# Batch 0's last inverse stage moves into the hand-written order of the transform's last three steps

## Chip, cores and metric

The kernel runs on one NeuronCore of a Trainium2 chip. The metric is device microseconds of one execution, lower is better. TensorE (PE) multiplies, VectorE (DVE) and ScalarE (ACT) take results out of PSUM and do elementwise work, GpSimd (POOL) does one subtraction, and SyncE (SP) issues all DMA transfers. Each engine works through its own instructions in order, and SP's queue is also in order: an instruction that waits holds up everything behind it on its engine.

## What is computed

```python
def _attn_ref(x, w_r, w_i, b_r, b_i):            # x: 8 x 3136 x 256
    X = np.fft.rfft(x, axis=1)
    Yr = X.real @ w_r - X.imag @ w_i + b_r
    Yi = X.real @ w_i + X.imag @ w_r + b_i
    Yr = np.sign(Yr) * np.maximum(np.abs(Yr) - 0.01, 0.0)     # Yi the same
    return np.fft.irfft(Yr + 1j * Yi, n=3136, axis=1)

def _moe_ref(x, w_in, conv_w, w_out):            # w_in: 256 x 1024
    h = np.maximum(x @ w_in, 0.0)
    conv = sum(conv_w[k] * shifted(h, k) for k in range(3))   # 3 taps along the sequence
    return (h * sigmoid(conv)) @ w_out

out = _moe_ref(_attn_ref(x, ...), ...)
```

## The kernel before

There are two parts. **The transform** splits the Fourier transform of length 3136 = 49 x 64 into two matmul stages each way. Stage 1 transforms blocks of the input and goes through DRAM (`sc1`). The rest is a pipeline over 50 items (`n_it`), an item being a batch and a group of four frequencies. In step `it` of the loop, PE does stage 2 of item `it` (`stage2`, 16 matmuls into `ps_s2`), the complex mix of item `it-1` (`mix`, 36 matmuls into `ps_mx0..2`), and stage 3 of item `it-3` (`stage3`, 12 matmuls into `ps_s3`). Each operand is split into a high and a low part, so DVE and ACT make pairs (`fh`/`fl`, `sh`/`sl`) between the matmuls. `threshold` of item `it-2` is a chain ACT `r`, DVE `v`, ACT `sh`, POOL `sl`, which stage 3 then reads. Stage 3's result is copied by ACT to `z1` and stored by SP to DRAM (`sc2`). The loop runs three steps past the last item to drain: `range(n_it + 3)`. The order of PE, DVE and ACT in this loop is the order in which the code is written (`manual_schedule`); SP, and everything after the loop, is ordered by a scheduler when the kernel is built.

**Stage 4**, the last inverse stage, makes a batch in eight pieces (`stage4`, n = 0 to 7). A piece loads two blocks `z2` from `sc2` (two DMAs of 200 KB), does 32 matmuls of 64x49 (they are 64 in the trace), and puts the result into a batch's `yh` (ACT, L520) and `yl` (DVE, L521). `new_y` clears the two edge columns of `yh` and `yl` by four memsets (L497, L498). There are two such pairs, `y_a` for even and `y_b` for odd batches.

**The FFN** runs over 28 chunks of 896 positions (two halves of 448), each with eight blocks f of the hidden size. `up` (L533) makes `ps_h`, ACT's relu gives `h`, then the taps `c` (ACT L540 or DVE L538, then DVE L542 twice), sigmoid (ACT L543), product (DVE L544) and the pair `gh`/`gl`. `down` (L561) accumulates four blocks later into `acc`. Stage 4 of the next batch is put between the blocks, a piece at f = 1, 4 and 7.

In this version the transform's pools stand in one stack `ab`, which is closed before stage 4's pools (`zio` with three `z2` buffers, `psh` with two PSUM buffers of two banks, shared by stage 4 and `ps_h`) are opened in the same memory. All eight pieces of batch 0 and the first two of batch 1 are written ahead of the FFN; the other six of batch 1 go between its blocks.

Of the kernel before, what the change touches and what calls it, by code (L numbers as in the profile page):

```python
# [100 lines left out]
def spectral_ffn_kernel(ctx: ExitStack, tc: tile.TileContext, x, w_r, w_i, b_r, b_i,  # L101
# [19 lines left out]
    with ExitStack() as ab:  # L121
        stg = ab.enter_context(tc.tile_pool(name="stg", bufs=1))
        wbp = ab.enter_context(tc.tile_pool(name="wbp", bufs=2))
        s1p = ab.enter_context(tc.tile_pool(name="s1p", bufs=2))
        c1 = ab.enter_context(tc.tile_pool(name="c1", bufs=1))
        a2p = ab.enter_context(tc.tile_pool(name="a2p", bufs=3))
        cmx = ab.enter_context(tc.tile_pool(name="cmx", bufs=1))
# [257 lines left out]
        with tc.tile_pool(name="hx", bufs=1, reuse_waits="tile") as hx:  # L385
# [22 lines left out]
        with tc.issue_after(ld.ins):  # L408
# [5 lines left out]
        ab.enter_context(tc.manual_schedule(engines={mybir.EngineType.PE}))
        ab.enter_context(tc.issue_after(ld.ins))
        wkf, wk, cab, io = [ab.enter_context(tc.tile_pool(name=nm, bufs=n, reuse_waits="tile"))
                            for nm, n in (("wkf", 2), ("wk", 2), ("cab", 1), ("io", 2))]
# [8 lines left out]
        ab.enter_context(tc.manual_schedule(engines={mybir.EngineType.DVE, mybir.EngineType.Activation}))  # L426
        for it in range(n_it + 3):
# [45 lines left out]
            if 0 <= it - 3 < n_it:  # L473
                stage3(*items[it - 3], ss.pop(it - 3))
# [18 lines left out]
    def new_y(b):
        y = [(y_a, y_b)[b % 2].tile([P, NT, SW], F32R, name=nm) for nm in ("yh", "yl")]
        for q in y:
            qf = q.bitcast(F32)
            nc.vector.memset(qf[:, :, 0:1], 0.0)  # L497
            nc.vector.memset(qf[:, :, S + 1:S + 2], 0.0)  # L498
        return y

    def stage4(b, n, y):

        js, t = slice(n // NT * JG, (n // NT + 1) * JG), n % NT
        z2 = zio.tile([P, JG, P], F32, name="z2")
        z2v = sc2[b].rearrange("(j o c) u e -> o (c u) j e", o=2, c=2)
        for o in range(2):
            nc.sync.dma_start(z2[o * R2:o * R2 + KI], z2v[o, :, js, t * P:(t + 1) * P])
        ps = psh.tile([P, 2, 512], F32, name="ps_s4", tag="ps_h")
        for j in range(JG):
            for o in range(2):  # L510
                rows = slice(o * R2, o * R2 + KI)
                for c in range(2):
                    half = slice(c * R2, (c + 1) * R2)
                    nc.tensor.matmul(ps[half, o, j * R:(j + 1) * R], z2[rows, j, half], i2[rows, :], start=(j == 0), stop=(j == JG - 1),  # L514
                                     skip_group_check=True)
        src = ps[:, :, 0:JG * R].rearrange("p o (j m) -> p o m j", j=JG)

        def view(q):
            return q[:, t, 1:S + 1].rearrange("p (m o j) -> p o m j", o=2, j=H)[:, :, :, js]
        nc.scalar.copy(view(y[0]), src)  # L520
        nc.vector.tensor_tensor(view(y[1]), src, view(y[0].bitcast(F32)), op=ALU.subtract)  # L521
# [69 lines left out]
    n_st = NCH * NF
    for st in range(n_st + LAG):
        if st < n_st:
            ci, f = divmod(st, NF)
            hv = [divmod(2 * ci + a, NH) for a in range(2)]
            if f == 0:
                nb = hv[1][0] + 1
                if nb < B and nb not in ys and hv[0][0] == hv[1][0]:
                    ys[nb] = new_y(nb)
                    todo = [(nb, jg) for jg in range(NPC)]  # L600
            gs[st] = up(f, [(ys[b], a * CH) for b, a in hv])
            if todo and f in (1, 4, 7):
# [29 lines left out]
```

## Time and profile before

| | |
|---|---|
| median of 3 runs | 1738.86 us (1737.77 to 1741.54) |
| the profiled execution | 1738.14 us, of which its span 1736.3 us |
| mean granted TensorE clock | 0.985 |
| PE busy | 1690.5 us (97%) |
| DVE busy | 1471.0 us (85%) |
| ACT busy | 1198.4 us (69%) |
| POOL busy | 118.6 us (7%) |

Times in the profile are microseconds from the span's start. A row of a timeline gives start, duration, engine, line, operation, output and inputs, and in brackets how long the engine had been idle and what ended that. The chain of work that ended last is followed back from the last instruction, at each step to what released it. A row of the table by windows gives, for a stretch of time, the busy time of each engine with its instructions in parentheses, then the clock that PE was granted (1.00 is full), the mean busy share of the 16 DMA engines and the GB/s they moved. Waits are put down to the last of the things waited for.

### The profile page before, as it was taken

The page shows a single profiled execution, that of the slowest core. Times are in us where ns is not written, and L with a number is a line of the kernel's source. Part 1 is how long each engine was busy: PE and PEld are TensorE (multiplying, and loading weights), DVE is VectorE, ACT ScalarE, POOL GpSimd, SP SyncE. Part 2 cuts the span into 40 slices and gives each one's busy share as a digit, 9 for nine tenths or more (in the row PEclk, how much of TensorE's full clock was granted, in tenths as well). Part 3 has the DMA queues.
Part 4 walks back from the last instruction along what each step waited for, and adds up shares of the span by engine and source line. Part 5 has one row for each costly group of instructions (what it writes and reads, how often), then busy time and mean ns, then how long its engine had stood idle before and what let it go on. Part 6 is the DMA issues. An engine that isn't in the chain of part 4 may idle for free.

```text
span 1736.3 us, 35086 instructions
## 1 busy us (share of the span) xinstructions
PE 1690.5 (97%) x14944; PEld 1552.5 (89%) x14944; DVE 1471.0 (85%) x1757; ACT 1198.4 (69%) x1565; POOL 118.6 (7%) x54
## 2 busy tenths in 40 slices
PE   5999999999997999999999999999999999999999
PEld 2778888888986999999999999999999999999998
DVE  2788988898993988888888898888888888888887
ACT  2567677767663877777777677777777777777776
POOL 0122222222230000000000000000000000000000
PEclk7999999999996999999999999999999999999999
DMA  7877777667435110111111111111101111100001
GB/s 229 256 236 243 229 227 239 223 203 250 142 106 130 39 41 22 31 51 51 52 53 53 38 41 51 51 41 51 51 22 42 51 51 42 51 22 22 22 22 43
DMA packets 134604, 165.87 MB, mean 96 GB/s; under 512 B 9166, under 2 KB 112590, under 8 KB 134448
## 3 DMA queue, kind: packets, MB, share of 16 engines
q1 hardware_dynamic: 134448, 163.62, 30.7%
q8 instruction: 118, 1.93, 0.5%
q14 instruction: 38, 0.31, 0.1%
HBM read 86.01 MB, written 77.59 MB: 94 GB/s over the span
## 4 chain that ended last, share of the span: by engine, by line
PE 93%; DMA 4%; DVE 2%; issue 1%; ACT 1%; SPq 0%; DVEq 0%; ACTq 0%
PE acc L561 32%; PE ps_h L533 32%; PE ps_mx L328 11%; PE ps_s L256 5%; PE ps_s L300 5%; PE ps_s L514 4%; PE ps_s L360 3%; DMA z<-sc 1%; DMA wm_raw<-in_w_i_dram 1%; DMA t<-in_fwd_dram 1%; DVE v L336 0%; DMA sc<-a 0%; PE ps_s1h L273 0%; DMA xr<-in_x_dram 0%; DVE p L332 0%
## 5 line engine op out<-in xcount | busy, mean ns | idle before, releaser
L561 PE MATMUL acc<-wout,gh 128*128 128x256 f32 x3136 | 567.7, 281 | 1.5 <-ACT gh L547 1.5
L533 PE MATMUL ps_h<-yh,win 128*128 128x450 f32 x1792 | 550.4, 368 | 0.0
L542 DVE SCALAR_TENSOR_TENSOR c<-h,cw,c 128x896 f32<-128x896 f32 x448 | 513.4, 1148 | 26.7 <-ACT c L540 24.5
L561 PEld LDWEIGHTS acc<-wout,gh 128*128 128x128 f32 x3136 | 491.3, 188 | 10.4 <-ACT gh L547 1.9
L561 PE MATMUL acc<-wout,gl 128*128 128x256 f32 x1568 | 437.0, 280 | 0.0
L533 PEld LDWEIGHTS ps_h<-yh,win 128*128 128x128 f32 x1792 | 339.2, 189 | 25.8
L535 ACT ACTIVATE h<-ps_h 128x900 f32<-128x900 f32 x224 | 207.1, 925 | 209.9 <-PE ps_h L533 209.9
L533 PE MATMUL ps_h<-yl,win 128*128 128x450 f32 x896 | 329.7, 368 | 0.0
L544 DVE TENSOR_TENSOR c<-h,c 128x896 f32<-128x896 f32 x224 | 243.9, 1089 | 70.1 <-ACT c L543 69.6
L561 PEld LDWEIGHTS acc<-wout,gl 128*128 128x128 f32 x1568 | 293.6, 188 | 0.1
L548 DVE TENSOR_TENSOR gl<-c,gh 128x896 fp32r<-128x896 f32 x224 | 243.2, 1089 | 41.4 <-ACT gh L547 40.5
L547 ACT CAST gh<-c 128x896 fp32r<-128x896 f32 x224 | 211.6, 945 | 60.9 <-DVE c L544 60.5
L543 ACT ACTIVATE c<-c 128x896 f32<-128x896 f32 x224 | 214.0, 955 | 52.8 <-DVE c L542 51.8
L328 PE MATMUL ps_mx<-wmix_hi,fl 128*128 128x256 f32 x600 | 185.1, 308 | 2.7 <-DVE fl L310 2.7
L328 PE MATMUL ps_mx<-wmix_hi,fh 128*128 128x256 f32 x600 | 183.5, 306 | 0.7 <-DVE v L336 0.5
L533 PEld LDWEIGHTS ps_h<-yl,win 128*128 128x128 f32 x896 | 169.6, 189 | 11.1
L540 ACT ACTIVATE c<-h,cw 128x896 f32<-128x896 f32 x168 | 175.1, 1042 | 1.8
L328 PE MATMUL ps_mx<-wmix_lo,fh 128*128 128x256 f32 x600 | 168.4, 281 | 0.0
L350 POOL TENSOR_TENSOR sl<-v,sh 128x1024 fp32r<-128x1024 f32 x50 | 118.4, 2368 | 407.7 <-PE ps_s L360 249.0
L336 DVE TENSOR_TENSOR v<-ps_mx,p 64x512 f32<-64x512 f32 x200 | 137.4, 687 | 2.9
L300 PEld LDWEIGHTS ps_s<-t,a 128*128 128x128 f32 (+1 forms) x800 | 99.4, 197 | 37.0 <-issue 26.3
L328 PEld LDWEIGHTS ps_mx<-wmix_hi,fh 128*128 128x128 f32 x600 | 113.2, 189 | 19.1 <-issue 17.4
(84 smaller groups left out, 1861.0 us busy)
## 6 DMA issues: line engine op xcount, KB each, us to landing
z<-sc SPq DMA_DIRECT2D x128, 200.0 KB
xr<-in_x_dram SPq DMA_DIRECT2D x63, 392.0 KB
a<-sc SPq DMA_DIRECT2D x48, 512.0 KB
sc<-z SPq DMA_DIRECT2D x48, 512.0 KB
out_dram<-o SPq DMA_DIRECT2D x27, 896.0 KB
sc<-a SPq DMA_DIRECT2D x56, 392.0 KB
sc<-ha SPq DMA_DIRECT2D x8, 392.0 KB
win_bits<-in_moe_w_in_dram SPq DMA_DIRECT2D x4, 512.0 KB
```

Source lines behind the costliest of these rows:

```text
L300: nc.tensor.matmul(ps[:, k], a2[0:rows, k, t * P:(t + 1) * P], t2[0:rows, u, :], start=(k == 0), stop=(k == UG - 1), skip_group_check=True)
L328: nc.tensor.matmul(ps[c][:, k, :], lt, rh, start=(n == 0), stop=(n == len(mm) - 1))
L336: nc.vector.tensor_tensor(v[dst, :, k, :], ps[c][src], p1[src, c], op=ALU.add)
L533: nc.tensor.matmul(ps[:, a, 0:CH + 2], lt, rh, start=(n == 0), stop=(n == len(mm) - 1))
L535: nc.scalar.activation(h, ps[:, :, 0:CH + 2], AF.Relu)
L540: nc.scalar.mul(c, h[:, :, 0:CH], cw[:, 0, f:f + 1])
L542: nc.vector.scalar_tensor_tensor(c, h[:, :, k:k + CH], cw[:, k, f:f + 1], c, op0=ALU.mult, op1=ALU.add)
L543: nc.scalar.activation(c, c, AF.Sigmoid)
L544: nc.vector.tensor_tensor(c, h[:, :, 1:CH + 1], c, op=ALU.mult)
L547: nc.scalar.copy(gh, c)
L548: nc.vector.tensor_tensor(gl, c, gh.bitcast(F32), op=ALU.subtract)
L561: nc.tensor.matmul(acc[m // 2][:, m % 2, :], lt[:, sl], rh[:, f, :], start=(f == 0 and n == 0 and m % 2 == 0), stop=(f == NF - 1 and n == ...
```

## The change

The transform's pools are put on two sides of SBUF and PSUM. Those that are done when the last stage 2 is done (weights' staging, stage 1, `a2`; `ps1`, `ps2`) are on the left and closed early; the others (mix, threshold, stage 3) are on the right. Stage 4's `zio` (now five buffers) and `y_a` take the early pools' place during step `n_it - 1`, and SP gets the loads of pieces 0 to 4 there. Piece 0 is put between the mix's matmuls of that step, with a PSUM tile `ps_z` of its own. The loop runs to `n_it + 1`; what the last two steps did is written out behind it, with pieces 1 to 7 between. Batch 1's first two pieces go into the FFN's order with the other six. `ps_mx1` is now the lowest of the mix's three PSUM banks, in the place that `psh`'s second buffer will take. `y_b`'s `yl` now lies over `z1`, `i1_lo` and the mix's weights; before, it lay over `i1_lo`, `z1` and the end of `i1_hi`. All addresses in SBUF move, and the scratch for dynamic DMA is 4 KB instead of the default.

```diff
+ZB = 5
...
+    def load_z2(zio, b, n):
+        js, t = slice(n // NT * JG, (n // NT + 1) * JG), n % NT
+        z2 = zio.tile([P, JG, P], F32, name="z2")
+        z2v = sc2[b].rearrange("(j o c) u e -> o (c u) j e", o=2, c=2)
+        for o in range(2):
+            nc.sync.dma_start(z2[o * R2:o * R2 + KI], z2v[o, :, js, t * P:(t + 1) * P])
+        return z2
+
+    def stage4(z2, n, y, ps):
...
+        nc.scalar.copy(view(y[0]), src)
+        yield None
+        nc.vector.tensor_tensor(view(y[1]), src, view(y[0].bitcast(F32)), op=ALU.subtract)
+        yield None
...
+    with ExitStack() as late:
+        early, ps_early, ps_mid, ps_late, order = [late.enter_context(ExitStack()) for _ in range(5)]
...
-        ps1 = ab.enter_context(tc.tile_pool(name="ps1", bufs=1, space=PSUM))
-        ps2 = ab.enter_context(tc.tile_pool(name="ps2", bufs=2, space=PSUM))
-        psm = ab.enter_context(tc.tile_pool(name="psm", bufs=1, space=PSUM))
-        psa = ab.enter_context(tc.tile_pool(name="psa", bufs=1, space=PSUM))
+        ps1 = ps_early.enter_context(tc.tile_pool(name="ps1", bufs=1, space=PSUM))
+        ps2 = ps_early.enter_context(tc.tile_pool(name="ps2", bufs=2, space=PSUM))
+        psa = ps_late.enter_context(tc.tile_pool(name="psa", bufs=1, space=PSUM, side="right"))
+        psm = ps_mid.enter_context(tc.tile_pool(name="psm", bufs=1, space=PSUM, side="right"))
...
-        for it in range(n_it + 3):
+        zs = []
+        for it in range(n_it + 1):
...
             some(two, 2)
+            if it == n_it - 1:
+                early.close()
+                zio, y_a = pool("zio", ZB), pool("y_a")
+                zs += [load_z2(zio, 0, n) for n in range(ZB)]
+            if it == n_it:
+                some(head, 1)
...
+            if it == n_it - 1:
+                ps_early.close()
+                first_psh = ExitStack()
+                ps_z = first_psh.enter_context(tc.tile_pool(name="psz", bufs=1, space=PSUM, reuse_waits="tile"))
+                ys = {0: new_y(y_a)}
+                head = stage4(zs[0], 0, ys[0], ps_z.tile([P, 2, 512], F32, name="ps_z"))
+                some(head, 1)
             some(mx, 64)
...
+        first_psh.close()
+        ps_mid.close()
+        psh = pool("psh", 2, space=PSUM)
+        def to_y(n):
+            q = stage4(zs[n], n, ys[0], psh.tile([P, 2, 512], F32, name="ps_s4", tag="ps_h"))
+            yield next(q)
+            if n + ZB < NPC:
+                zs.append(load_z2(zio, 0, n + ZB))
+            yield from q
+        zs.append(load_z2(zio, 0, ZB))
+        some(to_y(1), 2)
+        stage3(*items[n_it - 3], ss.pop(n_it - 3))
+        some(to_y(2), 2)
+        th = threshold(vs.pop(n_it - 1)[0])
+        ss[n_it - 1] = next(th)
+        q = to_y(3)
+        some(q, 1)
+        some(th, 1)
+        some(q, 1)
+        some(th, 1)
+        stage3(*items[n_it - 2], ss.pop(n_it - 2))
+        some(to_y(4), 2)
+        some(to_y(5), 2)
+        some(to_y(6), 2)
+        some(to_y(7), 2)
+        stage3(*items[n_it - 1], ss.pop(n_it - 1))
...
-    for jg in range(NPC):
-        with tc.high_priority(offset=HP):
-            stage4(0, jg, ys[0])
-    ys[1] = new_y(1)
-    for jg in range(2):
-        stage4(1, jg, ys[1])
-    todo = [(1, jg) for jg in range(2, NPC)]
+    todo = []
...
-    nc = _bacc.Bacc("TRN2", target_bir_lowering=False, num_devices=1)
+    nc = _bacc.Bacc("TRN2", target_bir_lowering=False, num_devices=1, dynamic_dma_scratch_size=4096)
```

How the instructions then stand is shown at three places. On PE, in words: before, the last mix is followed by stage 3 of the third-last, second-last and last item, with the 32 matmuls of batch 0's pieces mixed in two at a time, and then two pieces of batch 1. Now it is the last mix, piece 1, stage 3 of the third-last item, pieces 2 and 3, stage 3 of the second-last, pieces 4 to 7, stage 3 of the last item, and then the FFN. From the FFN's first matmul on, PE's order is the same but for the two pieces, which come in the third chunk.

ACT from the threshold of the second-last item on (`sh`; `r` is a threshold's first step, `z` the copy of stage 3's result, `yh` a piece of stage 4). Before:

```order
L349 CAST sh<-v 128x1024
L362 COPY z_5724<-ps_s_5711 128x1024
L345 ACTIVATE r<-v,small 128x1024
L349 CAST sh<-v 128x1024
L520 CAST yh<-ps_s_5855 128x2x49x8
L520 CAST yh<-ps_s_5817 128x2x49x8
L362 COPY z_5747<-ps_s_5734 128x1024
L520 CAST yh<-ps_s_5893 128x2x49x8
L520 CAST yh<-ps_s_5931 128x2x49x8
L362 COPY z_5763<-ps_s_5750 128x1024
```

Now, from the threshold of the third-last item on:

```order
L394 CAST sh<-v 128x1024
L151 CAST yh<-ps_z 128x2x49x8
L407 COPY z_5729<-ps_s_5716 128x1024
L390 ACTIVATE r<-v,small 128x1024
L394 CAST sh<-v 128x1024
L151 CAST yh<-ps_s_5795 128x2x49x8
L407 COPY z_5846<-ps_s_5833 128x1024
L151 CAST yh<-ps_s_5849 128x2x49x8
L390 ACTIVATE r<-v,small 128x1024
L151 CAST yh<-ps_s_5891 128x2x49x8
L394 CAST sh<-v 128x1024
L407 COPY z_5942<-ps_s_5929 128x1024
```

Before, no piece stood ahead of the last item's `sh`, and two ahead of the copy of the second-last item's stage 3 (`z_5747`). Now four pieces stand ahead of that copy (`z_5942`), and piece 3 stands between `r` and `sh` of the last threshold.

DVE at the clearing of batch 1's `yh` and `yl` (MEMSET). Before:

```order
L521 TENSOR_TENSOR yl<-ps_s_5893,yh 128x2x49x8
L521 TENSOR_TENSOR yl<-ps_s_5931,yh 128x2x49x8
L497 MEMSET yh 128x2
L498 MEMSET yh 128x2
L497 MEMSET yl 128x2
L498 MEMSET yl 128x2
L521 TENSOR_TENSOR yl<-ps_s_5969,yh 128x2x49x8
```

Now:

```order
L153 TENSOR_TENSOR yl<-ps_s_6050,yh 128x2x49x8
L589 TENSOR_SCALAR c<-h,cw 128x896
L160 MEMSET yh 128x2
L161 MEMSET yh 128x2
L160 MEMSET yl 128x2
L161 MEMSET yl 128x2
L593 SCALAR_TENSOR_TENSOR c<-h,cw,c 128x896 x3
L595 TENSOR_TENSOR c<-h,c 128x896
```

The four memsets stood between batch 0's fourth and fifth piece; now they stand behind all eight, between the first two instructions of the FFN's first block. The memset of `yl` waits, then as now, for the last store of `z1`, over which `yl` lies.

SP's queue from the third-last store of stage 3's result on (`sc<-z`, 512 KB) with the loads of pieces (`z<-sc`, two of 200 KB to a piece; `sc_0` is batch 0's, `sc_1` batch 1's). Before:

```order
L364 DMA sc_7_72<-z_5724 128x1024
L507 DMA z_5928<-sc_0_65 50x8x128
L507 DMA z_5966<-sc_0_65 50x8x128
L507 DMA z_5928<-sc_0_65 50x8x128
L507 DMA z_5966<-sc_0_65 50x8x128
L364 DMA sc_7_72<-z_5747 128x1024
L507 DMA z_6004<-sc_0_65 50x8x128
L507 DMA z_6042<-sc_0_65 50x8x128
L507 DMA z_6004<-sc_0_65 50x8x128
L507 DMA z_6042<-sc_0_65 50x8x128
L364 DMA sc_7_72<-z_5763 128x1024
```

Now:

```order
L409 DMA sc_7_72<-z_5846 128x1024
L134 DMA z_5883<-sc_0_65 50x8x128 x2
L134 DMA z_6184<-sc_1_66 50x8x128 x2
L409 DMA sc_7_72<-z_5942 128x1024
L134 DMA z_6297<-sc_1_66 50x8x128 x2
L134 DMA z_6477<-sc_1_66 50x8x128 x2
L134 DMA z_6607<-sc_1_66 50x8x128 x2
L134 DMA z_6789<-sc_1_66 50x8x128 x2
L409 DMA sc_7_72<-z_6098 128x1024
```

Between the last two stores stood the loads of two pieces of batch 0; now it is four pieces of batch 1, which the FFN needs later.

More of the change, by code (lines that the diff above doesn't have):

```diff
@@ L118, in spectral_ffn_kernel @@
     mlam, warm = small[:, 0:1], small[:, 1:2]
[L121 to L127, printed above, removed]
+    JG = 8
+    NPC = H // JG * NT
@@ new lines, in stage4, with view @@
+    def stage4(z2, n, y, ps):
+        js, t = slice(n // NT * JG, (n // NT + 1) * JG), n % NT
+        for j in range(JG):
+            for o in range(2):
+                rows = slice(o * R2, o * R2 + KI)
+                for c in range(2):
+                    half = slice(c * R2, (c + 1) * R2)
+                    nc.tensor.matmul(ps[half, o, j * R:(j + 1) * R], z2[rows, j, half], i2[rows, :], start=(j == 0), stop=(j == JG - 1),
+                                     skip_group_check=True)
+        src = ps[:, :, 0:JG * R].rearrange("p o (j m) -> p o m j", j=JG)
+        def view(q):
+            return q[:, t, 1:S + 1].rearrange("p (m o j) -> p o m j", o=2, j=H)[:, :, :, js]
+        nc.scalar.copy(view(y[0]), src)
+        yield None
+        nc.vector.tensor_tensor(view(y[1]), src, view(y[0].bitcast(F32)), op=ALU.subtract)
+        yield None
@@ new lines, in new_y @@
+    def new_y(yp):
+        y = [yp.tile([P, NT, SW], F32R, name=nm) for nm in ("yh", "yl")]
+        for q in y:
+            qf = q.bitcast(F32)
+            nc.vector.memset(qf[:, :, 0:1], 0.0)
+            nc.vector.memset(qf[:, :, S + 1:S + 2], 0.0)
+        return y
+    with ExitStack() as late:
+        early, ps_early, ps_mid, ps_late, order = [late.enter_context(ExitStack()) for _ in range(5)]
+        stg = early.enter_context(tc.tile_pool(name="stg", bufs=1))
+        wbp = early.enter_context(tc.tile_pool(name="wbp", bufs=2))
+        s1p = early.enter_context(tc.tile_pool(name="s1p", bufs=2))
+        c1 = early.enter_context(tc.tile_pool(name="c1", bufs=1))
+        a2p = early.enter_context(tc.tile_pool(name="a2p", bufs=3))
+        pool("top", 1, late, side="right").tile([P, 80], F32, name="pad")
+        cmx = late.enter_context(tc.tile_pool(name="cmx", bufs=1, side="right"))
@@ L262, in stage1_head @@
         def stage1_head(xs, b=0):
-            with tc.tile_pool(name="ha", bufs=1, reuse_waits="tile") as ha:
+            with tc.tile_pool(name="ha", bufs=1, side="right", reuse_waits="tile") as ha:
                 for jc, xr in enumerate(xs):
@@ L269, in stage1_head @@
                         if k < 3:
-                            ps = psm.tile([K1, 2, D], F32, name="ps_s1h", tag=f"ps_mx{k}")
+                            ps = psm.tile([K1, 2, D], F32, name="ps_s1h", tag=f"ps_mx{(1, 0, 2)[k]}")
                         else:
@@ L315, in mix @@
             fh, fl = xs
-            ps = [psm.tile([K2, UG // 2, D], F32, name=f"ps_mx{c}") for c in range(3)]
+            ps = {c: psm.tile([K2, UG // 2, D], F32, name=f"ps_mx{c}") for c in (1, 0, 2)}
             p1 = wk.tile([K2, 2, UG // 2, D], F32, name="p1", bufs=1)
@@ L384, in spectral_ffn_kernel @@
         load_f1()
-        with tc.tile_pool(name="hx", bufs=1, reuse_waits="tile") as hx:
+        with tc.tile_pool(name="hx", bufs=1, side="right", reuse_waits="tile") as hx:
             xh = []
@@ L413, in spectral_ffn_kernel @@
                 ask()
[L414 to L417, printed above, removed]
+        order.enter_context(tc.manual_schedule(engines={mybir.EngineType.PE}))
+        order.enter_context(tc.issue_after(ld.ins))
+        io, cab, wk, wkf = [pool(nm, n, late, side="right") for nm, n in (("io", 2), ("cab", 1), ("wk", 2), ("wkf", 2))]
         cab.tile([P, 56], F32, name="pad")
-        wkf.tile([P, 56], F32, name="pad", bufs=1)
         wk.tile([P, 72], F32, name="pad", bufs=1)
+        wkf.tile([P, 8], F32, name="pad", bufs=1)
         i1_hi = cab.tile([K2, U + 2, KQ], F32R, name="i1_hi")
@@ L425, in spectral_ffn_kernel @@
         xs, vs, ss, i1s = {}, {}, {}, {}
-        ab.enter_context(tc.manual_schedule(engines={mybir.EngineType.DVE, mybir.EngineType.Activation}))
-        for it in range(n_it + 3):
+        order.enter_context(tc.manual_schedule(engines={mybir.EngineType.DVE, mybir.EngineType.Activation}))
+        zs = []
+        for it in range(n_it + 1):
             xs[it], vs[it - 1] = [], []
@@ L472, in spectral_ffn_kernel @@
                 held[:] = [0] * (next(background, None) == "act")
-            if 0 <= it - 3 < n_it:
+            if it == n_it:
+                break
+            if it >= 3:
                 stage3(*items[it - 3], ss.pop(it - 3))
@@ L493, in new_y @@
[L493 to L521, printed above, removed]
@@ L523, in up @@
+    y_b.tile([P, 32], F32, name="pad")
+    pso = pool("pso", space=PSUM)
     def up(f, halves):
@@ L603, in spectral_ffn_kernel @@
                 b, jg = todo.pop(0)
-                stage4(b, jg, ys[b])
+                for _ in stage4(load_z2(zio, b, jg), jg, ys[b], psh.tile([P, 2, 512], F32, name="ps_s4", tag="ps_h")):
+                    pass
         if st >= LAG:
```

20 lines of the change are left out of this document (7 added, 13 removed).

## Prediction, made before the changed kernel ran

> **What bounds the kernel now.** I read the page first: how much of the time PE works, and where not.
>
> ```profile
> PE 1690.5 (97%) x14944; PEld 1552.5 (89%) x14944; DVE 1471.0 (85%) x1757; ACT 1198.4 (69%) x1565; POOL 118.6 (7%) x54
> PE   5999999999997999999999999999999999999999
> PEclk7999999999996999999999999999999999999999
> ```
>
> PE is the bound almost everywhere; besides the start there is one dent, the thirteenth slice (521 to 564 us). That is the place of the change. The table by windows shows it, with a stretch of the FFN for comparison (PE busy first, then PEld, DVE, ACT, POOL; behind them granted clock, DMA share and GB/s):
>
> ```profile
> 510.00:515.00 5.00, 3.67 (x28) 3.16 (x27) 4.94 (x8) 1.96 (x2) 1.92 (x1) 1.00 0.07 27
> 525.00:530.00 5.00, 2.48 (x86) 2.23 (x89) 1.72 (x2) 1.52 (x2) 1.52 (x1) 0.76 0.82 212
> 540.00:545.00 5.00, 2.63 (x75) 2.34 (x69) 1.95 (x4) 1.70 (x2) 0.00 (x0) 0.50 0.36 89
> 555.00:560.00 5.00, 5.00 (x43) 4.52 (x38) 0.97 (x1) 1.23 (x2) 0.00 (x0) 0.66 0.73 158
> 570.00:650.00 80.00, 80.00 (x813) 75.67 (x812) 73.69 (x74) 60.23 (x69) 0.00 (x0) 1.00 0.14 38
> ```
>
> Up to 515 DVE has no gap (4.94 of 5.00). Then nobody is full, and PE runs at half clock. From 570 on PE has no gap. The chain of waits says what the dent is made of:
>
> ```profile
> 509.26 1.30 PE ps_s L360 x11
> ...
> 523.08 5.38 DMA z<-sc
> 528.51 3.08 PE ps_s L514 x95
> ...
> 532.36 5.66 DMA z<-sc
> ...
> 541.44 4.68 DMA z<-sc
> ...
> 555.80 6.32 PE ps_h L533 x24
> ...
> 567.35 1.22 PE acc L561 x8
> 568.57 4.93 PE ps_h L533 x24
> ...
> 575.14 1.08 PE ps_s L514 x64
> ```
>
> Stage 4 alternates load (4.7 to 5.7 us) and matmuls (3.08 us at half clock), since three `z2` buffers come free only when PE has read them. The FFN starts at 555.80; its first two blocks take 6.32 us cold (4.93 us warm, at 568.57), and its first `down` starts at 567.35. From there PE is the chain, so what the change is worth is the shift of that `down`, plus what is added to PE behind it.
>
> **The new order, step by step.** Up to 510 us the orders are the same. Durations of what follows, by groups (mean ns), and DVE's own timeline:
>
> ```profile
> L521 DVE TENSOR_TENSOR yl<-ps_s,yh 128x784 fp32r<-128x784 f32 x64 | 61.8, 971 | 18.9 <-ACT yh L520 18.9
> L347 DVE SCALAR_TENSOR_TENSOR v<-v,r 128x1024 f32<-128x1024 f32 x50 | 61.0, 1220 | 1.3 <-ACT r L345 1.3
> L520 ACT CAST yh<-ps_s 128x784 fp32r<-128x784 f32 x64 | 58.4, 920 | 21.1 <-PE ps_s L514 21.1
> L345 ACT ACTIVATE r<-v,small 128x1024 f32<-128x1024 f32 x50 | 58.4, 1167 | 2.6 <-DVE v L336 2.5
> L349 ACT CAST sh<-v 128x1024 fp32r<-128x1024 f32 x50 | 52.6, 1051 | 69.7 <-DVE v L347 69.4
> L350 POOL TENSOR_TENSOR sl<-v,sh 128x1024 fp32r<-128x1024 f32 x50 | 118.4, 2368 | 407.7 <-PE ps_s L360 249.0 <-ACT sh L349 152.7 <-PE ps_s L300 5.9
> L362 ACT COPY z<-ps_s 128x1024 f32<-128x1024 f32 x50 | 50.5, 1010 | 25.2 <-PE ps_s L360 22.9 <-issue 1.2 <-DMA sc<-a 0.5
> ```
>
> ```profile
> 511.73 0.69 DVE L310 TENSOR_TENSOR fl<-d,fh 128x512 fp32r<-128x512 f32 x1
> 512.33 2.81 DVE L336 TENSOR_TENSOR v<-ps_mx,p 64x512 f32<-64x512 f32 x4
> 515.24 1.29 DVE L332 TENSOR_TENSOR p<-ps_mx,bias 128x512 f32<-128x512 f32 x2
> ...
> 540.90 0.06 DVE L497 MEMSET yl<- 128x2 f32 x1 [6.25 <-DMA sc<-z]
> ...
> 561.36 2.34 DVE L542 SCALAR_TENSOR_TENSOR c<-h,cw,c 128x896 f32<-128x896 f32 x2
> ```
>
> Neighbours on an engine overlap by about 0.1 us, so in a row each counts so much less. A piece is 1.08 us on PE, a stage 3 is 1.4 us (1.30 for 11 of its 12).
>
> Piece 0 costs nothing: PE has its 1.08 us free, since the next mix waits for `fl` (done 512.42) in any case. Its `yl` puts 0.97 us on DVE, which is full. DVE then reads: `v` to 515.3, `yl` 0 to 516.25, `p` to 517.4, threshold `v` to 518.6, the last four `v` to 521.3. PE: last mix done 516.85, piece 1 to 518.0, third-last stage 3 to 519.4. Piece 2 needs `psh`'s second buffer, over `ps_mx1`, so it waits for DVE's 521.3 and ends at 522.5. Now ACT and DVE set the pace: ACT `yh` 2 to 523.4, `r` to 524.5, `yh` 3 to 525.3; DVE `yl` 2 to 524.4, threshold `v` to 525.8, `yl` 3 to 526.7. PE: piece 3 to 523.6, stage 3 to 525.0, piece 4 to 526.1, piece 5 (after `yl` 3) to 527.85. ACT: `sh` to 526.9, `z` to 527.75, `yh` 4 to 528.55, `yh` 5 to 529.4; `yl` 4 to 529.55. PE: piece 6 from there to 530.75, piece 7 to 531.85, last stage 3 to 533.25. POOL's `sl` (2.37 us behind `sh`: 522.2 and 529.4) is never last. The FFN starts at 533.3 (both `psh` buffers are read by 533.8). That is 22.5 us earlier. The loads don't delay it: the first loads were issued from 480.15 on (row below), some 0.4 to 0.7 us each, and pieces 0 to 4 need no more than 490 (an estimate: ten at that pace, and some waits); piece 7's, the latest, is issued at 522.6 (when piece 2 is read) and is needed at 530.7; the longest load in the chain took 5.66.
>
> PE has 11.8 us of work in these 16.4, 72%, as in 510 to 515 (3.67 of 5.00), where the clock stayed 1.00. So I take the first two blocks warm: 4.93 instead of 6.32, done at 538.2, **23.9 us earlier**.
>
> **The new wait.** Relu of the first block is done at 536.8 and DVE's first tap at 537.55. Then come the memsets of batch 1, which wait for the last `z` store. It was the same wait that held DVE for 6.25 us to 540.90, with nothing urgent behind it. Now all of the FFN's DVE work is behind it. The store is issued when ACT has copied the last stage 3, at 534.35, behind four pieces of batch 1.
>
> ```profile
> 480.15 3.49 SPq L507 DMA_DIRECT2D z<-sc  x5
> ...
> 535.53 0.34 SPq L364 DMA_DIRECT2D sc<-z  x1
> 551.00:557.00 6.00, 5.29 (x131) 4.92 (x132) 2.00 (x3) 1.82 (x2) 0.00 (x0) 0.50 0.73 159
> 533.00:540.00 7.00, 4.31 (x109) 3.87 (x110) 1.46 (x4) 1.29 (x2) 0.00 (x0) 0.74 0.75 191
> ```
>
> The first row is SP's issue of the first pieces, the second of the last store. The first window holds loads of pieces alone: 159 GB/s, so 2 x 204.8 KB take 2.6 us. The second holds two pieces and then the store: 1.34 MB at 191 GB/s. The store issued at 535.53 was in at 540.90, 5.4 us later and 0.9 behind the last byte. Now: the second-last store is issued at 527.8 and moves from about 529.5; behind it come four pieces (4 x 2.6 = 10.4) and the last store. A store adds about 1.4 us (the second window's 7.0, less 2 x 2.6 for its pieces, less 0.4 at its edges). So the last byte moves at 529.5 + 10.4 + 2.8 = 542.7, and the store is in at 543.6, the memsets done at 543.7. Bounds: 539.7, if the queue is no longer than before (534.35 + 5.4), and 546, if the mix moves at 191 GB/s and everything ahead is 1.5 us late. I take 543.7, since the loads ahead are four and not two. DVE so waits **6.2 us** (2.2 to 8.5).
>
> From the taps' start to the first `down` it was 567.35 - 561.36 = 6.0 us; that chain through DVE and ACT is the same. First `down`: 543.7 + 6.0 = 549.7 instead of 567.35. PE meanwhile does a piece and one more block, to 541.8, and then has nothing for 7.9 us.
>
> **The clock.** Windows of 3.4 us, laid where the granted clock changes:
>
> ```profile
> 517.60:521.00 3.40, 1.97 (x67) 1.64 (x67) 2.73 (x5) 2.48 (x3) 2.07 (x1) 1.00 0.14 55
> 521.00:524.40 3.40, 2.75 (x95) 2.49 (x87) 1.23 (x1) 2.05 (x3) 0.54 (x2) 1.00 0.41 143
> 524.40:527.80 3.40, 0.99 (x32) 0.74 (x32) 1.86 (x2) 2.12 (x3) 2.12 (x1) 0.98 0.78 179
> 527.80:531.20 3.40, 2.69 (x94) 2.69 (x96) 0.00 (x0) 0.00 (x0) 0.00 (x0) 0.50 0.59 181
> 555.00:558.40 3.40, 3.40 (x35) 3.04 (x30) 0.97 (x1) 0.91 (x1) 0.00 (x0) 0.51 0.73 154
> ```
>
> After 1.97 busy of 3.40 the clock stayed, after 0.99 it was halved, and after a full window it came back. So 7.9 us of idling halve it, and `down` begins cold. Before, PE worked without a gap from 553.85 and was warm at 558.4: 4.6 us at half speed, which is 2.3 us lost (at most twice 3.4, so 3.4 lost; nothing, if the wait is short). The Trainium skill, "TensorE: Matmul & The Clock Gate", section "Part 1: The HAM clock gate", has the same window of about 3.4 us, free-running, but lets only an idle window halve the clock. The trace is stricter: 0.99 busy did not save it. By the page the stretch of pieces, with no gap over 2.1 us, could not lose its clock at all, and the second rival below would have no chance.
>
> **Added to PE behind the first `down`:** two pieces of batch 1 in the third chunk, 2 x 1.08 = 2.2 us, in full, since PE has no gap there. Their 0.97 and 0.92 us on DVE and ACT lie in their gaps (73.69 and 60.23 of 80).
>
> **Sum:** -22.5 (FFN starts earlier) - 1.4 (warm blocks) + 6.2 (memset) + 2.3 (clock) + 2.2 (pieces) = **-13.2 us**. The profiled execution was 1738.14, so 1724.9; the median is 0.7 above it, so 1725.6. At nothing I cost: piece 0 on PE (covered by the wait for `fl`; without it 1.08 us); the new addresses and the scratch, which change no instruction; the earlier loads of pieces 2 to 4 (1.2 MB more around 490, with 10 us to spare).
>
> **Rivals.** (1) The store is in sooner. If no longer behind than before, 539.7, then DVE waits 2.2 and PE is idle for 3.9 us, which may keep the clock: -22.5 - 1.4 + 2.2 + 2.2 = -19.5, 1719.4. For it: store and loads together reached 191 GB/s, not 159. Against: twice the loads ahead. (2) The clock falls between the pieces. There PE waits for DVE and ACT about 2 us at a time, and one window with a third of work would do. Then three pieces cost 1 us more each (3.08 for 95 matmuls, against 1.08 for 64) and the first blocks 1.4: -13.2 + 4.4 = -8.8, 1730.0. Against: 1.97 of 3.40 was enough. (3) Slower than before. All tiles lie elsewhere, and if that slowed DVE in the FFN, DVE could become the bound:
>
> ```profile
> L542 DVE SCALAR_TENSOR_TENSOR c<-h,cw,c 128x896 f32<-128x896 f32 x448 | 513.4, 1148 | 26.7 <-ACT c L540 24.5
> ```
>
> DVE has 6.3 of 80 us free, so up to 8.6% more on each of its instructions is covered; every per cent above adds 0.01 x 0.92 x 1180 us = 11 us. From 9.8% on that eats the 13.2 us; at 11% it is 26 us, 1752. Nothing in the trace shows a duration that depends on the address.
>
> **Chances.** Forecast 0.50, (1) 0.24, (2) 0.18, (3) 0.03, and 0.05 that (2) and a late store come together, some 1734 to 1737. The range reaches from (1) to (2) with a us or so on each side for the spread of runs and for 0.05 us here and there in the steps: 1718.5 to 1731.5. A measurement here can tell 0.2%, 3.5 us. Faster by more: 0.93; within: 0.04; slower: 0.03.
>
> **What would show it.** Right: first FFN matmul near 533; in its first block a DVE memset that waited about 6 us for the store; PE idle for about 8 us before the first `down` near 550, then half clock for some 4 us; third chunk 2.2 us longer. Wrong: no wait at the memset (1); clock 0.50 between 518 and 533 (2); longer DVE means in the FFN (3); or a piece that waits for its load, which I excluded.

## The result, and the profile after

The changed kernel takes 1725.22 us (median of 4 runs, 1723.02 to 1726.18) against 1738.32 before: ratio 0.9923 [0.9902, 0.9944], 13.1 us faster. The forecast was 1725.6 us. The profiled execution took 1724.63 us. One execution, the profiled one of the run `again` below, was in a disturbed state and took 3954 us; no trace of it is used.

The page after, first the same lines that were shown of before:

```profile
PE 1686.4 (98%) x14944; PEld 1548.2 (90%) x14944; DVE 1470.7 (85%) x1757; ACT 1199.6 (70%) x1565; POOL 118.7 (7%) x54
PE   5999999999998999999999999999999999999998
PEclk8999999999998999999999999999999999999999
```

The dent in the thirteenth slice is an 8 instead of a 7. The windows of the stretch (PE, PEld, DVE, ACT, POOL busy, then granted clock, DMA share, GB/s):

```profile
520.00:525.00 5.00, 3.32 (x133) 3.06 (x131) 3.66 (x5) 3.79 (x5) 2.36 (x1) 0.81 0.65 194
525.00:530.00 5.00, 5.00 (x99) 4.78 (x96) 2.42 (x3) 3.31 (x5) 2.11 (x1) 0.51 0.71 169
530.00:535.00 5.00, 2.48 (x139) 2.20 (x135) 2.93 (x3) 2.62 (x3) 0.25 (x1) 0.84 0.76 201
535.00:540.00 5.00, 5.00 (x67) 4.82 (x68) 0.98 (x1) 1.37 (x2) 0.00 (x0) 0.50 0.71 155
570.00:650.00 80.00, 80.00 (x874) 75.32 (x873) 72.29 (x72) 59.17 (x71) 0.00 (x0) 1.00 0.20 55
```

PE was given half clock for much of 523 to 540, which the forecast had only as its second rival. The chain of work that ended last, from the third-last stage 3 (L405) to the first `down` (L612):

```profile
518.88 1.61 PE ps_s L405 x12
520.49 1.67 issue
522.15 2.92 PE ps_s L145 x128
525.07 2.86 PE ps_s L405 x12
527.93 1.94 PE ps_s L145 x64
...
531.86 1.48 PE ps_s L145 x75
533.34 1.52 issue
534.87 1.76 PE ps_s L145 x40
...
537.85 6.36 DMA z<-sc
544.21 1.31 issue
545.52 0.06 DVE yl L160
...
551.03 1.22 PE acc L612 x8
```

and DVE's and SP's timelines around the last `z` store (L409) and batch 1's memsets (L160):

```profile
529.88 9.13 SPq L134 DMA_DIRECT2D z<-sc  x8
540.58 0.34 SPq L409 DMA_DIRECT2D sc<-z  x1
543.30 0.69 DVE L589 TENSOR_SCALAR c<-h,cw 128x896 f32<-128x896 f32 x1 [4.74 <-ACT h L586]
545.52 0.06 DVE L160 MEMSET yl<- 128x2 f32 x1 [1.51 <-issue]
```

So the alternation of loads and matmuls is gone, as the change says. But the last store went out at 540.58 and not at 534.35, DVE waited 1.5 us for it and not 6.2, the first block of the FFN was not 22.5 us earlier but 16.5, and the first `down` came at 551.03 (forecast 549.7) with a warm PE. The chain puts the memset's wait down to a load (`z<-sc`) that was in at 544.21; the last of the store's own landings is at 545.41, 0.1 us ahead of the memset, and `free_store` below shows that the store is what it waited for. The total agreed; its terms did not. Two theories were open. **C**: what counts is PE's own lateness, so each us lost at half clock in the stretch is lost to the end, and the agreement is luck. **F** (a floor): the first `down` follows the landing of the last store, whose time is set by the loads around it, and PE may be early or late ahead of it at no price.

Single executions also differ before the change is reached: the last `fl` starts at 511.73 before and at 512.47 here (510.22 to 512.47 in all the profiles below), and keeps that offset from 250 us on. So places in the stretch are given as distances from that `fl`. `down` stands for the first one:

| kernel | clock below 1.00 in the stretch | first FFN matmul | memset's wait | `down` | from `down` to the end |
|---|---|---|---|---|---|
| before | most of it | +44.0 | | +55.6 | 1169.0 |
| forecast | no | +21.6 | 6.2 | +38.0 | 1173.5 |
| after | 13.7 us | +26.8 | 1.5 | +38.6 | 1171.8 |
| `after_again` | 6.8 | +24.1 | 3.2 | +37.1 | 1173.3 |
| `mx2_low` | 10.2 | +24.7 | 2.5 | +38.1 | 1174.5 |
| `twice` | 10.2 | +26.5 | 0.5 | +37.6 | 1171.8 |
| `zb3` | 10.2 | +28.0 | none | +39.1 | 1171.8 |
| `hold` | no | +21.5 | 10.4 | +38.7 | 1174.0 |
| `late_b1` | 6.8 | +24.4 | 0.8 | +34.9 | 1171.8 |
| `free_store` | 3.4 | +22.9 | none | +33.4 | 1171.8 |
| `free_again` | 6.8 | +24.2 | none | +34.5 | 1171.8 |
| `free_hold` | 3.4 | +24.6 | none | +35.0 | 1171.8 |
| `all_three` | 13.7 | +26.1 | none | +36.5 | 1171.8 |

The rest of the document argues from this table; its columns are read from the timelines of each profiled execution, the clock from the records of the granted clock, which change in steps of 3.41 us. "None" means that the memset did not wait for a store.

### The profile page after: what moved, and what is told of

It reads as the page before. It is cut to its first block, busy times and chain, and to the rows that moved or that the text cites. A ratio compares the mean times of both kernels' runs of the same rounds, so it can differ in the third digit from the quotient of the medians.

```text
span 1722.9 us, 35081 instructions
## 1 busy us (share of the span) xinstructions
PE 1686.4 (98%) x14944; PEld 1548.2 (90%) x14944; DVE 1470.7 (85%) x1757; ACT 1199.6 (70%) x1565; POOL 118.7 (7%) x54
## 4 chain that ended last, share of the span: by engine, by line
PE 93%; DMA 2%; DVE 2%; issue 1%; ACT 0%; SPq 0%; DVEq 0%; ACTq 0%
PE acc L612 33%; PE ps_h L584 32%; PE ps_mx L373 11%; PE ps_s L301 5%; PE ps_s L345 5%; PE ps_s L145 4%; PE ps_s L405 4%; DMA t<-in_fwd_dram 1%; DMA sc<-a 0%; DMA z<-sc 0%; DVE v L381 0%; DMA sc<-ha 0%; DVE fl L351 0%; DMA a<-sc 0%; DVE p L377 0%
## 5 line engine op out<-in xcount | busy, mean ns | idle before, releaser
L612 PE MATMUL acc<-wout,gh 128*128 128x256 f32 x3136 | 567.8, 281 | 2.5 <-ACT gh L598 2.5
L584 PE MATMUL ps_h<-yh,win 128*128 128x450 f32 x1792 | 549.7, 368 | 0.0
L593 DVE SCALAR_TENSOR_TENSOR c<-h,cw,c 128x896 f32<-128x896 f32 x448 | 513.2, 1147 | 26.5 <-ACT c L591 24.3
L612 PEld LDWEIGHTS acc<-wout,gh 128*128 128x128 f32 x3136 | 490.8, 188 | 11.4 <-ACT gh L598 2.9
L612 PE MATMUL acc<-wout,gl 128*128 128x256 f32 x1568 | 436.8, 280 | 0.0
L612 PEld LDWEIGHTS acc<-wout,gl 128*128 128x128 f32 x1568 | 293.6, 188 | 0.1
```

Source lines behind the costliest of these rows:

```text
L584: nc.tensor.matmul(ps[:, a, 0:CH + 2], lt, rh, start=(n == 0), stop=(n == len(mm) - 1))
L593: nc.vector.scalar_tensor_tensor(c, h[:, :, k:k + CH], cw[:, k, f:f + 1], c, op0=ALU.mult, op1=ALU.add)
L612: nc.tensor.matmul(acc[m // 2][:, m % 2, :], lt[:, sl], rh[:, f, :], start=(f == 0 and n == 0 and m % 2 == 0), stop=(f == NF - 1 and n == ...
```

## Experiments

**The changed kernel again, and three single edits.**

> The changed kernel once more, beside the next three on one chip: 1725 us, ratio 0.992 to the kernel before. Both theories below expect in its trace what the first trace had: half clock from about 523 to 530 and 533 to 540, first FFN matmul near 539, the memset of batch 1's yl waiting 1 to 2 us for the last store, first down near 551. If the clock falls in other windows here, the stretch of pieces should move by some us, but theory F (floor: DMA is busy from 520 to 544 with batch 1's loads, so the last store lands near 544 to 546 however early it is issued, and the first down follows 5.5 to 6 us later) expects the first down to stay at 549 to 551.5; theory C (clock: what the stretch loses at half clock is lost to the end) expects the first down to move with the first FFN matmul.

Measured: 1725.31 us, ratio 0.9925 [0.9911, 0.9938], the same as in the first measurement. What the two theories expected of its trace is left to `after_again` below.

```diff
-    ... f"ps_mx{(1, 0, 2)[k]}" ...        for c in (1, 0, 2)}
+    ... f"ps_mx{(2, 0, 1)[k]}" ...        for c in (2, 0, 1)}
```

> Only the mix's three PSUM banks change places: ps_mx2 (read first by DVE) lies in the lowest, so piece 2 waits for the p of the last mix instead of its last v. Piece 2 should start right behind the third-last stage 3, 1.6 us earlier, and the window in which the clock fell (about 1.75 us busy of 3.4) is then busy for 2.8 or more. Theory C: the clock stays 1.00 to 533, the first FFN matmul comes at 534 to 535 instead of 539, and the time falls by 4 to 5 us (1720 to 1721). Theory F: the same in the stretch, but the memset then waits 5 to 6 us instead of 1.5, PE idles longer before the first down, and the time falls by 0 to 1.5 us (1724 to 1725).

Measured: 1723.74 us (1720.04 to 1726.26), 0.9914 [0.9901, 0.9928]. The wait of 1.67 us ahead of piece 2 is gone, and a wait of 1.55 us ahead of piece 3, for DVE's `yl`, stands in its place: DVE sets the pace, whichever bank is free. The clock fell here too (10.2 us of the stretch), so the run doesn't decide between the theories. Its profiled execution shows the forecast's clock term: PE idle for 3.5 us ahead of the first `down`, and then cold. Windows of the clock's own 3.41 us:

```profile
545.74:549.15 3.41, 0.76 (x4) 0.36 (x2) 3.41 (x4) 1.90 (x3) 0.00 (x0) 1.00 0.30 83
549.15:552.57 3.42, 2.58 (x10) 2.54 (x11) 3.42 (x4) 3.38 (x4) 0.00 (x0) 0.50 0.00 0
```

```diff
         pool("top", 1, late, side="right").tile([P, 80], F32, name="pad")
+        io = pool("io", 2, late, side="right")
...
-        io, cab, wk, wkf = [... for nm, n in (("io", 2), ("cab", 1), ("wk", 2), ("wkf", 2))]
+        cab, wk, wkf = [... for nm, n in (("cab", 1), ("wk", 2), ("wkf", 2))]
```

The stores' buffers `io` now stand where no tile of batch 1 comes.

> z1's two buffers lie at the top of SBUF, so that batch 1's yl waits for the second-last store (landed near 533) and not for the last. The order of all engines is the same. Both theories: no wait at the memset, DVE's taps follow at 544.0, first down 1.5 us earlier, 1723.7 us. If the time does not fall by 1 to 2 us, the wait at the memset is not what holds the first down.

Measured: 1718.83 us (1717.19 to 1719.85), 0.9887 [0.9873, 0.9900]. 6.5 us less than the changed kernel, where 1.5 were expected by both theories: the edit takes away more than the wait that one trace showed. The chain no longer passes through a DMA:

```profile
533.31 5.06 PE ps_h L585 x24
...
543.60 1.22 PE acc L613 x8
```

```diff
-                for _ in stage4(load_z2(zio, b, jg), jg, ...
+                with tc.issue_after(last.ins) if b == 1 and 1 <= jg <= 4 else ExitStack():
+                    z2 = load_z2(zio, b, jg)
+                for _ in stage4(z2, jg, ...
```

where `last` is the last `z` store: four of batch 1's loads go behind it on SP.

> The loads of batch 1's pieces 1 to 4 are issued behind the last store instead of ahead of it. Theory F: the store lands about 3 us after its issue instead of 4.9, DMA is idle in parts of 530 to 540, the memset does not wait, first down 1.5 us earlier: 1723.7; if the pause of 1.65 us that PE makes in piece 7 without any semaphore comes from full DMA queues, it goes too, and the time is 1722. Theory C: the store's landing matters by 1.5 us at most, and the pause stays: 1723.7 to 1725.

Measured: 1720.45 us (1717.29 to 1721.55), 0.9893 [0.9878, 0.9908], 4.9 us less than the changed kernel. SP's timeline and the chain:

```profile
528.17 9.81 SPq L409 DMA_DIRECT2D sc<-z  x2
538.07 10.40 SPq L134 DMA_DIRECT2D z<-sc  x9
```

```profile
537.64 3.01 DMA sc<-z
540.66 0.76 issue
541.41 0.06 DVE yl L160
```

The first row holds both last stores; the last one was issued at 537.64. The chain ends its move 3.0 us later, and the memset starts 0.76 us after that; the last of the store's landings is at 541.30, 29.3 us after `fl`. In the changed kernel that landing is at 545.41, 4.8 us behind its issue and 32.9 after `fl`. Part of this is PE's doing, since the store was issued 25.6 us after `fl` here and 28.1 there; beside `after_again` below (issued at 25.4, in at 31.5) the loads ahead of the store are worth 2.5 us of its landing. Both edits at the store help by more than C allows (1.5 us), and by more than F had put down too (1.5, or 3 if the pause went).

**The parts of the change, and all edits together.**

> The changed kernel with the 64 matmuls of pieces 1 and 5 written twice (the second time over the first, so the output is the same): 2 x 1.08 us more work for PE, laid into gaps where it waited, to keep the clock up between the pieces. Theory C (what PE loses at half clock between 523 and 540 is lost to the end): the first FFN matmul comes at 22 to 23 us after `fl` instead of 26.8, and 3.5 to 4.5 us of it stay: 1720.5 to 1722. Theory F (a floor: the memset waits for the last store, which lands 31.5 to 33 us after `fl` whatever PE does, and the first `down` follows 5.5 later): DVE's memset waits 3 to 6 us, PE idles 4 us or more before the first `down`, and the time is 1723.5 to 1726. If the clock falls in spite of the added work, the run says nothing on either.

Measured: 1722.37 us (1720.98 to 1728.05), 0.9912 [0.9898, 0.9927]. The clock fell in spite of the added work, so by its own condition it says nothing.

> The changed kernel with three z buffers instead of five: the new order alone. Pieces 5 to 7 then have their loads issued only when pieces 2 to 4 are read (522 to 527), 4 to 6 us ahead of their need, and are 1 to 2 us late; but only three loads of batch 1, not five, stand ahead of or beside the last store. Theory F: the store lands no later than before, 1722 to 1725. Theory C (lateness of PE counts): 1726 to 1728.

Measured: 1724.04 us, 0.9917 [0.9903, 0.9931]: the order alone is worth all of the change. Pieces 5 and 7 wait for their loads,

```profile
521.44 4.50 DMA z<-sc
...
527.19 6.40 DMA z<-sc
```

and the FFN begins 28.0 us after `fl`, later than in any other profile of the new order. The memset no longer waits, so here PE's lateness has reached the floor: `down` comes 0.5 us later than in the changed kernel's first profile and 2.0 later than in `after_again`, and then runs warm. The time doesn't show it; it is in F's range.

> The kernel before with five z buffers and the small scratch, and its old order: the buffers alone. If the stretch of pieces was bound by the loads (five loads of 2.6 us between 520 and 556), two of them fall away and it is 1732 to 1735. If it was bound by the order (the pieces behind the last steps, on ACT and DVE), 1737 to 1739.

Measured: 1733.05 us (1731.65 to 1733.79), 0.9967 [0.9955, 0.9980]: the buffers alone, with the small scratch, are worth 5.9 us. The two gains, 14.9 and 5.9, don't add up to the 13.1 of both.

> The changed kernel with the three single edits together: the lower bank free for piece 2, the stores' buffers at an address of their own (no memset waits for a store), and batch 1's loads 1 to 4 issued only behind the last store. Theory F: with the floor gone only PE's own lateness counts, first `down` at FFN start plus 10.5: 1716 to 1718.5, some 1 to 2 us under `free_store`. Theory C alone: the same as `free_store`, 1718.5 to 1720. The pause of 1.4 to 1.6 us that PE made 75 matmuls into pieces 6 and 7 with no semaphore to wait for: if the full DMA queue makes it, it is gone here, since no load runs then; if not, it is here too, as in `mx2_low`.

Measured: 1721.35 us, 0.9902 [0.9888, 0.9915]. Both theories missed. No store is waited for, but piece 2 now runs alone, early, and PE then waits 1.6 us: the window there (1.99 us busy, row in the last section) halved the clock, and in this execution it stayed low for four windows (13.7 us), until about where the FFN began, at +26.1. `down` follows 10.5 us behind, as in `free_store`. With the store out of the way PE's lateness does count.

**Holding the clock.** Windows with many of the pieces' small matmuls had been followed by half clock. So 20 large ones (128x256), whose results are overwritten, were put into PE's waits:

```diff
+        def idle3(g, sh, times, ps=None):
+            ps = ps or psa.tile([KQ, UG, D], F32, name="ps_s3")
+            for k in [k for _ in range(times) for k in range(UG)]:
+                u = g * UG + k if g < NG else U + k % 2
+                nc.tensor.matmul(ps[:, k, :], i1_hi[:, u, :], sh[:, k, :], start=True, stop=True)
+            return ps
...
-        stage3(*items[n_it - 3], ss.pop(n_it - 3))
+        stage3(*items[n_it - 3], ss.pop(n_it - 3), times=2)
...
+        idle = idle3(items[n_it - 1][1], ss[n_it - 1][0], 3)
         some(to_y(6), 2)
...
-        stage3(*items[n_it - 1], ss.pop(n_it - 1))
+        stage3(*items[n_it - 1], ss.pop(n_it - 1), idle)
```

> The changed kernel with 20 further matmuls of stage 3's size (128x256), whose results are overwritten: 8 ahead of the third-last stage 3, and 12 ahead of piece 6, where PE waited for `yl`. They cost 0.12 us each and lie in waits, but for some 0.5 us. Windows of 3.41 us with 124 to 127 of the pieces' small matmuls and 2.38 to 2.40 us busy were followed by half clock, so it is the large ones that should hold it. Theory C (time at half clock is lost to the end): the first FFN matmul 22 to 23 us after `fl` instead of 26.8, and 1720.5 to 1721.5. Theory F (the memset waits for the last store, which lands 31.5 to 32.5 us after `fl` however early PE is): a memset wait of 3 to 5 us, the first `down` still 37 to 38 us after `fl`, PE idle for about 5 us ahead of it and cold after: 1723.5 to 1726.

Measured: 1726.15 us (1723.41 to 1727.03), 0.9924 [0.9912, 0.9936]. The clock held through the whole stretch, and the FFN began at 533.18, 5.3 us sooner after `fl` than in the changed kernel. Windows of the stretch, and of the wait that followed:

```profile
524.59:528.00 3.41, 2.86 (x133) 2.51 (x133) 2.03 (x2) 2.86 (x4) 1.00 (x1) 1.00 0.74 170
528.00:531.42 3.42, 3.27 (x132) 3.06 (x135) 1.86 (x2) 1.95 (x3) 1.39 (x1) 1.00 0.90 243
531.42:534.83 3.41, 3.41 (x45) 3.23 (x38) 1.93 (x4) 2.30 (x3) 0.00 (x0) 1.00 0.77 159
541.66:545.07 3.41, 0.34 (x2) 0.00 (x0) 0.91 (x4) 0.00 (x0) 0.00 (x0) 1.00 0.69 197
545.07:548.48 3.41, 0.00 (x0) 0.00 (x0) 3.37 (x4) 1.23 (x2) 0.00 (x0) 0.50 0.07 14
```

And nothing came of it. Timelines of ACT, SP, DVE and PE:

```profile
533.43 1.01 ACT L415 COPY z<-ps_s 128x1024 f32<-128x1024 f32 x1 [0.70 <-PE ps_s L413]
528.24 8.70 SPq L134 DMA_DIRECT2D z<-sc  x8
537.03 1.20 SPq L417 DMA_DIRECT2D sc<-z  x1
544.13 0.06 DVE L160 MEMSET yl<- 128x2 f32 x1 [10.37 <-issue]
550.35 2.08 PE L621 MATMUL acc<-wout,gh 128*128 128x256 f32 x8 [8.35 <-ACT gh L607]
```

The last `z` was ready at 534.4. SP was still issuing eight loads, 1.09 us each, and came to the store at 537.03; it was in at 543.9. DVE stood at the memset for 10.4 us, PE for 8.4, and the first `down` ran cold (2.08 us for eight, 1.22 in the changed kernel). C is refuted: 5.3 us of PE's time were given and `down` came at +38.7 instead of +38.6. F is near in both (1723.5 to 1726, and +37 to +38); only the memset's wait was longer than its 3 to 5 us. That it is the store that swallows PE's time, the next run shows.

> The same 20 matmuls, and the stores' buffers at an address of their own, so no memset waits for a store. C and F both have the first `down` 10.5 us after the first FFN matmul, 32.5 to 33.5 after `fl`: 1717 to 1719. The difference to `hold` is what the store costs once PE is in time: C gives 2 us or less, F 5 to 7.

Measured: 1718.79 us (1715.33 to 1720.86), 0.9884 [0.9869, 0.9898]: 7.4 us less than `hold` (C: 2 or less, F: 5 to 7), by nothing but the place of the stores' buffers. The profiled executions differ by 6.3 us: 3.7 are an earlier `down`, 2.2 a cold start that is gone, 0.3 lie ahead of `fl`. `down` came at +35.0 and not at the 32.5 to 33.5 that both theories expected, because the clock did not hold here: PE paused for 1.31 us inside piece 6 (last section), that window had 1.95 us busy, and the next was at half clock. So the large matmuls held the clock in one of two profiles.

> `free_store` once more. Its profiled run had only one window at half clock in the stretch of pieces, that of the changed kernel four. If that was chance of where the windows fell, its other runs lie between: 1721 to 1723. If it belongs to the kernel, 1718 to 1719.5.

Measured: 1720.03 us, 0.9893 [0.9878, 0.9908], between the two expectations. Its profile has two windows at half clock where `free_store` had one, and `down` at +34.5 instead of +33.4. So where the windows fall is partly chance, and worth about 1 us from one execution to the other; the gain is the kernel's.

> The changed kernel once more, beside the three others on one chip. 1725; its profile, if the windows fall otherwise, shows how much of the 1.5 us at the memset and of the 26.8 us from `fl` to the first FFN matmul belongs to that one execution: C gives a time that follows the first FFN matmul, F a first `down` 38 to 39 us after `fl` in any case.

Measured: 1723.89 us, 0.9918 [0.9905, 0.9932]. This execution of the changed kernel had half the time at half clock, an FFN 2.7 us sooner, and a memset that waited longer:

```profile
543.17 0.06 DVE L160 MEMSET yl<- 128x2 f32 x1 [3.24 <-issue]
548.68 1.88 PE L612 MATMUL acc<-wout,gh 128*128 128x256 f32 x8 [4.25 <-ACT gh L598]
545.52:548.93 3.41, 0.25 (x2) 0.25 (x3) 3.41 (x5) 2.99 (x4) 0.00 (x0) 1.00 0.00 0
548.94:552.35 3.41, 3.41 (x14) 3.19 (x14) 3.41 (x4) 2.99 (x4) 0.00 (x0) 0.50 0.00 0
```

Of the 2.7 us 1.4 reached `down` (+37.1, under the 38 to 39 that F had put down), and a cold start of 1.5 us (1173.3 against 1171.8) took them back.

**The best version** measured is the changed kernel with the stores' buffers at an address of their own: 1718.83 and 1720.03 us, 6.5 and 3.9 below the changed kernel in the same comparisons, 19.6 and 18.0 below before. The large matmuls on top of it change nothing that can be told (1718.79).

## Why the prediction came out right, step by step

- **Order up to the third-last stage 3, and piece 2's wait for `v`.** Right: stage 3 ends at 520.49 (forecast 519.4; 0.74 of the difference is this execution's offset), then 1.67 us until piece 2.
- **The FFN starts 22.5 us earlier.** The schedule is right when the clock stays: `hold` started it 21.5 us after `fl`, the forecast was 21.6. In the changed kernel's two profiles it was 26.8 and 24.1, since the clock fell. The step of this term that failed is "72% busy keeps the clock": a window with 2.40 of 3.42 us busy, 70%, was followed by half clock (next section).
- **First two blocks warm, -1.4.** Wrong in the first profile (the clock was low until 540.2), right in `hold` and `free_hold` (4.92 for 24). It makes no difference to `down` as long as the store is later.
- **The memset's wait, +6.2.** The wait was named rightly, and its end rightly too: the store in at 543.6 and memsets done at 543.7, 32.0 us after `fl`; measured 31.5 (`after_again`), 32.3 (`hold`), 32.9 (after). Only the length was another, 1.5 to 10.4, since it is what is left between the FFN's taps and that landing. In `hold` the memset stands ahead of the first tap, so its wait is longer by what the tap would have filled. One piece of the working was missing: it counted the time that the loads ahead of the store take to move, but none that SP takes to issue them. Loads at "0.4 to 0.7 us each" were the first ones; these eight took 8.0 to 10.5 us, 1.0 to 1.3 each, and in `hold` the store stood 2.6 us behind them on SP.
- **Cold after the idle time, +2.3.** By the execution: 0 in the first profile, 1.5 in `after_again`, 2.7 in `mx2_low`, 2.2 in `hold` (last column of the table, less 1171.8). It doesn't grow with the idle time ahead of `down`, which was 4.3, 3.5 and 8.4 us in these three; 2.5 us, in the first profile, cost nothing.
- **Two pieces in the third chunk, +2.2.** Behind `down` 2.8 us were added (1171.8 against 1169.0); 2.5 of them come between the `gl` of the second chunk's last block and that of the third's.
- **The second rival** (the clock falls between the pieces: +4.4, 1730.0) happened in both profiles of the changed kernel, and cost next to nothing. The mistake was to add it to the sum: a delay ahead of the store's landing isn't added to that landing, it is swallowed by it. By the same rule the 6.2 and the 2.3 were the price of being early, not terms of their own. That the sum held within 2 us was no luck: its paths run through the landing, and that was forecast to about 1 us. That it held to 0.4 us was luck: `down` came 0.6 us later after `fl` than forecast and `fl` itself 0.7 later, and the tail was 1.7 shorter, since PE was warm. And the delay of 5.2 us was about as much as the landing could swallow: the `z` store went out 5.5 us later after `fl` than forecast, and 1.2 us more of lateness (`zb3`) left the memset no wait.
- **The first rival** (the store in sooner, 1719.4) is near to what `late_b1` makes: in at 29.3 us after `fl` (the rival had 28.0), 1720.45. **The third** (addresses slow DVE) didn't happen: the taps in the FFN take 1147 ns on average, 1148 before.

## What to carry to other kernels

Before adding up gains along a chain, look for a wait further down that doesn't move with them: here a store's landing 32 us after `fl`, so that 5 us of a faster PE ahead of it were worth nothing, and 5 us of a slower one too, but no more than that. When the pools of two phases share addresses, the first write of the new phase can wait for the last transfer of the old; giving the two buffers of that transfer an address of their own was worth 4 to 7 us, a third to a half of what the whole change brought. To learn what a wait costs, don't read its length in one trace (1.5 us here); take its cause away.

## What the runs showed of the hardware

**Small matmuls hold the clock less than their busy time says.** Four windows of 3.41 us each, laid where the clock changes, three of the changed kernel and the last of `all_three`; the third kept the clock, the others were followed by half clock:

```profile
519.70:523.11 3.41, 1.73 (x71) 1.56 (x70) 3.29 (x5) 2.48 (x3) 2.36 (x1) 1.00 0.53 131
529.94:533.36 3.42, 2.40 (x135) 2.12 (x131) 1.95 (x2) 2.06 (x3) 0.31 (x1) 1.00 0.77 224
547.01:550.42 3.41, 1.50 (x8) 1.04 (x6) 3.41 (x4) 2.12 (x3) 0.00 (x0) 1.00 0.42 115
520.62:524.03 3.41, 1.99 (x71) 1.93 (x72) 3.33 (x4) 3.11 (x4) 1.30 (x1) 1.00 0.79 197
```

2.40 us, nearly all of the pieces' 50x64 matmuls with 49 columns, lost it, 1.50 us of the FFN's 128x128 ones with 450 columns kept it, and `hold`, with 12 matmuls of 256 columns added to such a window, kept it at 3.27. So busy time isn't the measure; what is (columns, rows, or work), these runs don't tell. Nor does 1.97 us of 3.40 (x67) always suffice, which kept the clock in the forecast's table: the last window has 1.99 (x71) and lost it. A full window at half clock doesn't always bring the clock back either, when 77 of its 84 matmuls are small ones:

```profile
523.12:526.53 3.41, 3.41 (x84) 3.32 (x76) 2.14 (x3) 2.74 (x3) 0.00 (x0) 0.50 0.72 234
```

The clock stayed at 0.50 for the window behind it, up to 529.94.

The Trainium skill, "TensorE: Matmul & The Clock Gate", section "Part 1: The HAM clock gate", has the length of the window right (3.41 us in these records), but that only an idle window lowers the clock does not hold here (2.40 us busy lost it).

**A pause of PE that waits for nothing.** In the changed kernel and in `all_three` PE stopped at the same matmul, the 76th of pieces 6 and 7, with no semaphore to wait for (so it did in `mx2_low`, for 1.23 us, and elsewhere in the pieces in `free_hold`, for 1.31, and in `twice`, for 1.67):

```profile
531.86 1.48 PE L145 MATMUL ps_s<-i,z 50*64 50x49 f32 x75 [1.00 <-DVE yl L153]
534.87 1.73 PE L145 MATMUL ps_s<-i,z 50*64 50x49 f32 x53 [1.52 <-issue]
```

```profile
529.25 2.37 PE L145 MATMUL ps_s<-i,z 50*64 50x49 f32 x75 [0.33 <-DVE yl L153]
533.09 1.74 PE L145 MATMUL ps_s<-i,z 50*64 50x49 f32 x53 [1.47 <-issue]
531.70:533.05 1.35, 0.00 (x0) 0.00 (x0) 0.83 (x1) 0.49 (x1) 0.00 (x0) 0.50 0.00 0
```

The last row is a window of `all_three`: DMA share 0.00 within the pause, so full queues, which the expectation had asked about, are not its cause. In the two profiles shown a packet of 16384 bytes on the queue of instructions had come in within 0.2 us ahead of it (532.42 to 533.30 in the changed kernel, where the pause begins at 533.34), and where PE waited for `yl` while that packet moved there was no pause (`free_store`, and the same kernel in `after_again`, where it moved from 527.69 to 528.96 and PE waited until 529.55). That PE had run out of instructions fits this; the Trainium skill, "Runtime: NRT & Kernel Launch", section "Instruction fetch mechanics", has blocks of 16 KiB, whose fetch it calls mostly hidden. No run took the fetch away, so the cause isn't shown.
